# Nystrom attention and two feed-forward layers on one core: new slots for the attention of batches 2 and 3, a later start for a decode, y stores from another queue

## The chip, the core and the metric

One NeuronCore of a Trainium2 chip runs the whole program. The time is the device time of one execution in microseconds (us). Engines named here: TensorE (PE; PEld is its loading of weights), VectorE (DVE), ScalarE (ACT), GpSimd (POOL) and SyncE (SP), which here only issues DMA transfers. An engine's name with a q (SPq, ACTq) is its queue of issues.

## The reference

```python
def _attn_ref(q, k, v):                   # 4 batches, 8 heads, 576 tokens, 64 wide
    q_lm = q.reshape(B, H, 32, S // 32, D).mean(axis=3); k_lm = ...
    A = sm(q, k_lm); Bm = sm(q_lm, k_lm); C = sm(q_lm, k)      # sm: scaled softmax
    Z = Bm.T / (norm1(Bm) * norminf(Bm) + 1e-06)
    for _ in range(6):
        Z = 2 * Z - Z @ Bm @ Z
    return A @ Z @ C @ v
x = attention as (2304, 512)
h = x @ w_in                              # 512 -> 2048
x = (h * tanh(softplus(h))) @ w_out       # 2048 -> 512
h = x @ w2_in                             # 512 -> 1024
ln = layernorm(h * softmax(h)) * g_ln
out = ln @ w2_out                         # 1024 -> 512
```

The weights are float64 and come in as pairs of 32-bit words: the kernel decodes them into float32 on ScalarE, GpSimd and VectorE, and splits the result into a high and a low part, so that a product takes three matmuls.

## The kernel before

**Stages.** The prologue computes batch 0's attention and begins to decode the first layer's weights. The main loop (L859) then runs over 64 pairs p of units; a unit is one of 16 column blocks (128 wide) of the first layer's 2048, for one of 8 chunks of 288 tokens. Two chunks are a batch: batch 1 begins at pair 16, batch 2 at pair 32, batch 3 at pair 48. Chunk 0 is cut in two, so there are nine segments. After the loop comes the second layer, 18 tiles of 128 tokens.

**A pair.** gemm1(p) (12 matmuls at L623, h<-AT,u) makes h of two units. mish(p) (L648) is ScalarE's activation; gsplit(p-1) (L656 on ScalarE, L658 on VectorE) splits its result. gemm2(p-3) (24 matmuls at L671, y<-gh,hl and y<-gl,hl) sums into four PSUM banks y. At the end of a segment, evac (L685) copies each of the four banks into one of two tiles ye on ScalarE (L688) and issues its store to the DRAM buffers yd or yp on ScalarE's queue (L689).

**Attention beside it.** attn(b, g) is a generator for batch b and four of the eight heads, with 17 steps. A pair calls slot() five times (the points in '1sa.u..t2..u' at L880), so pair p holds slots 5p+1 to 5p+5. PLAN (L600) gives each generator its first slot and the slots between its steps. The tiles of one generator are single buffers shared by all, and its result AT lies in a buffer that batch b-2 used. finish_w (L508) is its last step. When both generators of a batch are done, four u steps (u_step, L605: 16 matmuls at L612, copies at L615 on ScalarE and L616 on VectorE) multiply w tiles of the first layer into u tiles; each may run as soon as the batch before has used the old u tile for the last time (may_step, L854), at the two points 'u' of a pair. A u step takes both PSUM tiles "a" of the attention.

**Second layer's weights.** The fourth u step of batch 3 is the last reader of the w tiles. At the end of that pair (or of pair 47, if that is later) the code issues the loads of w2_in (decode2, L798, into the four w tiles), closes the attention's PSUM pool and gives its memory to a second h tile (ps_x). decode works in steps: L151 on GpSimd, L154 on ScalarE, L163 and L172 on VectorE, then the split at L222 (L225) and L231 (L234). tick() (L864) does these steps while `w2n < W2R * (u - w2u)`, with W2R = 0.6, where w2u is the unit at which the loads were issued. w2_out follows in the same way into the u tiles (L914, L921).

**Order.** Instructions are written in the order of these loops. A planner puts them into each engine's queue by its own estimate of when each is ready; the place in the text is a priority. Each engine then runs its queue in order. load_y (L813), which reads yd back for the second layer, is written for pair 61 and later.

Of the kernel before, what the change touches and what calls it, by code (L numbers as in the profile page):

```python
# [27 lines left out]
def nystrom_moe_kernel(  # L28
# [13 lines left out]
    V, A, PE, G, SP = nc.vector, nc.scalar, nc.tensor, nc.gpsimd, nc.sync  # L42

    B, _, _, SH = q.shape
# [6 lines left out]
    NG = H // HG  # L51
# [10 lines left out]
    N = CR * L  # L62
# [9 lines left out]
    yd = dram.tile([P, KD, NT], F32, name="yd")  # L72
    yp = dram.tile([P, KD, N], F32, name="yp")
# [523 lines left out]
    SB = 2  # L597
    XB = 1
    YB = 2
    PLAN = {(b, g): ((6, 19.2, 97, 117, 169, 212)[2 * b + g - 2], (1.6, 1.8, 1, 2.2, 0.5, 1.5)[2 * b + g - 2]) for b in range(1, B) for g in range(NG)}  # L600
    late, anchor, atl = [], [], []
    bank_n = [0, 0]
    done = 0
# [30 lines left out]
    def gemm1(p):  # L634
        pool = ps_x[0] if ps_x and p % 2 and p < U // 2 - 1 else ps_h
        h = pool.tile([P, 2, 512], F32, tag="h", name="h")
        for e in range(2):
            s_, i = units[2 * p + e]
            b, r = divmod(segs[s_][0] * CR, R)
            w = u_q(i // 4)[:, :, :, i % 4 * P:(i % 4 + 1) * P]  # L640
            o = slice(r * L, r * L + N)
            mm3(h[:, e, 0:N], [(w[:, x, g], aw[b, g][y][:, o]) for x, y in ((0, 0), (0, 1), (1, 0)) for g in range(NG)])
        hb[p] = h[:, :, 0:N]

    def mish(p):
        h = hb.pop(p)
        s = mp.tile([P, 2, N], F32, tag="s", name="s", bufs=SB)
        A.activation(out=s, in_=h, func=AF.Mish)  # L648
        gb[p] = s

    def gsplit(p, tick):
        s = gb[p]
        gh = mp.tile([P, 2, N], F32R, tag="gh", name="gh", bufs=GB)
        gl = mp.tile([P, 2, N], F32R, tag="gl", name="gl", bufs=GLB)
        for e in range(2):
            A.activation(out=gh[:, e], in_=s[:, e], func=AF.Copy)  # L656
            tick()
            V.tensor_tensor(out=gl[:, e], in0=s[:, e], in1=f(gh[:, e]), op=ALU.subtract)  # L658
            tick()
        gb[p] = (gh, gl)  # L660

    def gemm2(p):
        s_, i = units[2 * p]
        _, i0, i1 = segs[s_]
        if i == i0:
            yb[s_] = [ps_y.tile([P, 512], F32, tag=f"y{d}", name=f"y{d}") for d in range(KD)]
        gh, gl = gb.pop(p)
        rs = [(k, s, r, e) for k, (s, r) in enumerate((("h", gh), ("l", gh), ("h", gl))) for e in range(2)]

        def add(k, s, r, e, d):  # L670
            PE.matmul(yb[s_][d][:, 0:N], lhsT=w_out(s, i + e)[:, d * P:(d + 1) * P], rhs=r[:, e],  # L671
                      start=i == i0 and e == k == 0, stop=i + 2 == i1 and e == 1 and k == 2)

        if i == i0 or i + 2 == i1:
            for d in range(KD):
                for x in rs:
                    add(*x, d)
                if i + 2 == i1:
                    evac(s_, d)
        else:  # L680
            for x in rs:
                for d in range(KD):
                    add(*x, d)

    def evac(s_, d):  # L685
        c = segs[s_][0]
        t = mp.tile([P, N], F32, tag="ye", name="ye", bufs=YB)
        A.activation(out=t, in_=yb[s_][d][:, 0:N], func=AF.Copy)  # L688
        A.dma_start(out=yp[:, d] if s_ == 0 else yd[:, d, c * N:(c + 1) * N], in_=t)  # L689

    with ExitStack():
        make_identity(nc, ident)
# [22 lines left out]
        def w1_tick(n=1):  # L715
            nonlocal done, ticks
            for _ in range(n):
                if done < NU and (ticks < 7 or atl):
                    ticks += 1
                    with tc.issue_after(atl[-1].ins) if atl else nullcontext():  # L720
                        done = next(w1, 10 ** 6)

        tasks = []
        for b in range(1, B):
            for g in range(NG):
                at, gaps = PLAN[b, g]
                tasks.append([b, at, 0, gaps, attn(b, g)])
        now = 0

        def advance(x):  # L730
            with behind(2):
                if next(x[4], "end") == "end":
                    tasks.remove(x)
                    return False
            x[1] += x[3]
            x[2] += 1
            return True
# [3 lines left out]
        for g in range(NG):  # L741
            prep, e, c, t, a = attn(0, g)
            for nm, x in (("q", prep("q")), ("k", prep("k")), ("e", e()), ("c", c()), ("t", t), ("a", a())):
                ch[f"{nm}{g}"] = x
        for nm in PSEQ.split():
            if nm == "d":
                w1_tick(1)
            elif nm == "x":
                advance(tasks[0])
                tasks[0][1] = PLAN[1, 0][0]  # L750
            elif nm not in ch and nm[0] != "w":
# [15 lines left out]
        def slot():  # L767
            nonlocal now
            now += 1
            while ahead and free_tag():  # L770
                b, g, nm = ahead.pop(0)
                load(b, g, nm)
            if late:
                with behind(0):
                    if next(late[0], "end") == "end":
                        late.pop(0)
            for x in list(tasks):
                while x[1] <= now:
                    if not advance(x):
                        break  # L780

        def finish(b):
            for x in [x for x in tasks if x[0] <= b]:
                while advance(x):
                    pass
# [56 lines left out]
        def need(side, i):  # L842
            while done <= pos[side, i] and done < NU and (ticks < 7 or atl):
                w1_tick()

        def next_step():
            b, s = steps.pop(0)
            if b == 0:
                for i in range(4 * s, 4 * s + 4):
                    need("i", i)  # L850
            finish(b)
            u_step(b, s)

        def may_step(u):  # L854
            b, s = steps[0]
            return all((b, g) in aw for g in range(NG)) and (b == 0 or last_use[b - 1, s] < u) and \
                (b > 0 or done > max(pos["i", i] for i in range(4 * s, 4 * s + 4)))

        for p in range(U // 2):  # L859
            u = 2 * p + 1  # L860
            s_, i = units[u]
            c, i0, i1 = segs[s_]

            def tick():  # L864
                nonlocal w2n
                nonlocal k4
                if done < NU:
                    k4 += 1
                    want = t0 + (3 * NU + 3 - t0) * (p + k4 / 5) / DT
                    while ticks < want and done < NU:  # L870
                        w1_tick()
                elif w2 and w2n < W2R * (u - w2u):
                    w2n += 1
                    if next(w2[0], "end") == "end":
                        w2.pop(0)

            while steps and first_use[steps[0]] <= u:
                next_step()
            k4 = 0
            for x in '1sa.u..t2..u':  # L880
                if x == '1':
                    gemm1(p)
                elif x == 'a':
                    mish(p)
                elif x == 's' and p:
                    gsplit(p - 1, tick)
                elif x == 't':
                    tick()
                elif x == '.':
                    slot()  # L890
                elif x == 'u':
                    for _ in range(US):
                        if steps and may_step(u + 1):
                            next_step()
                elif x == '2':
                    while g2 <= p - LAG:
                        need("o", units[2 * g2 + 1][1])
                        gemm2(g2)
                        g2 += 1
            if u + 1 == (NCH - 2) * NF:  # L900
                finish(B)
                att_s.close()
                tr = ctx.enter_context(tc.tile_pool(name="tr", bufs=1))
            if tr is not None and not steps and not vi:
                vi[None] = None
                w2.append(decode2(vi_pairs()))
                w2u = u
                psa_s.close()
                if HX:
                    psx_s = ExitStack()  # L910
                    ps_x.append(psx_s.enter_context(tc.tile_pool(name="ps_x", bufs=1, space=PS, side="right")))
            if c == NCH - 1:
                if i == NH - 1:
                    w2.append(decode2(vo_pairs((0, 1))))  # L914
                if i == NF - 5:
                    load_y(0)
                if i == NF - 3:
                    split_y(0)
                    load_y(1)
# [151 lines left out]
```

## Time and profile before

| | us |
|---|---|
| median of 3 runs | 659.76 (659.3 to 661.57) |
| profiled execution | 659.22 |
| its span, first to last instruction | 657.4 |
| TensorE busy | 626.1 (95%) |
| VectorE busy | 384.1 (58%) |
| ScalarE busy | 313.6 (48%) |

The span is what the trace covers; the rest of the execution's time lies around it. A share of busy time is an average over the prologue, the main loop and the second layer, which have different limits, so the stages are read one by one.

### The profile page before, as it was taken

How to read it: one execution, taken by the hardware profiler on the slowest of the kernel's cores; microseconds unless marked ns; L12 is line 12 of the kernel's file. 1: busy time of each engine (PE TensorE's matmuls, PEld its weight loads, DVE VectorE, ACT ScalarE, POOL GpSimd, SP SyncE). 2: the span in 40 equal slices, each digit the busy share in tenths (PEclk: the TensorE clock that was granted, in tenths of full speed). 3: DMA queues.
4: the chain of work that ended last, by engine and by line, in shares of the span. 5: the costliest groups of instructions: out<-in, count | busy, mean ns of one | idle time of the engine just before them, and what ended most of it. 6: DMA issues, size and time to landing. Idle time of an engine off the chain costs nothing.

```text
span 657.4 us, 11835 instructions
## 1 busy us (share of the span) xinstructions
PE 626.1 (95%) x4808; PEld 528.1 (80%) x4808; DVE 384.1 (58%) x976; ACT 313.6 (48%) x580; POOL 41.6 (6%) x21
## 2 busy tenths in 40 slices
PE   5687899999999999999997999999999999999997
PEld 2345777889889878898875999997888888888886
DVE  5899998931737235413536713457966656666560
ACT  2379985543537245424635634536534343343431
POOL 2420000000000000000005201310000000000000
PEclk9768999999999999999997999999999999999999
DMA  8998040310212010101046103213111111110001
GB/s 324 396 408 328 1 130 16 110 37 28 82 37 92 19 37 1 38 1 37 1 119 197 46 1 131 99 65 101 49 48 49 33 49 48 44 53 17 17 32 50
DMA packets 30584, 55.43 MB, mean 84 GB/s; under 512 B 3649, under 2 KB 19009, under 8 KB 30529
## 3 DMA queue, kind: packets, MB, share of 16 engines
q1 hardware_dynamic: 25344, 49.36, 21.4%
q10 hardware_dynamic: 5184, 5.31, 2.4%
q8 instruction: 38, 0.62, 0.4%
q14 instruction: 18, 0.14, 0.1%
HBM read 44.63 MB, written 10.03 MB: 83 GB/s over the span
## 4 chain that ended last, share of the span: by engine, by line
PE 85%; ACT 5%; DVE 4%; DMA 3%; issue 1%; POOL 1%; SPq 0%; POOLq 0%; ACTq 0%; DVEq 0%
PE h L623 28%; PE y L671 28%; PE po L623 15%; PE pa L612 3%; PE pt L975 2%; PE pa L298 2%; PE pa L442 2%; PE pa L353 1%; PE pa L429 1%; DMA r<-in_moe_w_in_dram 1%; POOL r L151 1%; DMA scr_w<-in_k_dram 1%; DMA r<-in_moe_w_out_dram 1%; DVE r L163 1%; ACT L648 1%
## 5 line engine op out<-in xcount | busy, mean ns | idle before, releaser
L671 PE MATMUL y<-gh,hl 128*128 128x288 f32 x1024 | 166.2, 301 | 2.4 <-ACT hl L222 1.4
L671 PEld LDWEIGHTS y<-gh,hl 128*128 128x128 f32 x1024 | 144.5, 190 | 14.1 <-issue 8.1
L623 PE MATMUL h<-AT,u 128*128 128x288 f32 x768 | 123.0, 305 | 3.7 <-ACT s L648 1.8
L623 PEld LDWEIGHTS h<-AT,u 128*128 128x128 f32 x768 | 107.9, 192 | 15.1 <-ACT u L615 4.7
L658 DVE TENSOR_TENSOR gl<-s,gh 128x288 fp32r<-128x288 f32 x128 | 55.1, 467 | 110.5 <-ACT gh L656 48.2
L623 PE MATMUL h<-hl,yb 128*128 128x512 f32 x432 | 103.2, 394 | 0.3 <-DVE s L948 0.3
L623 PEld LDWEIGHTS h<-hl,yb 128*128 128x128 f32 x432 | 79.7, 188 | 17.1 <-issue 1.0
L671 PE MATMUL y<-gl,hl 128*128 128x288 f32 x512 | 89.6, 298 | 0.0
L623 PE MATMUL po<-hl,lh 128*128 128x512 f32 x288 | 89.1, 390 | 0.0
L671 PEld LDWEIGHTS y<-gl,hl 128*128 128x128 f32 x512 | 75.0, 189 | 4.2 <-issue 3.0
L656 ACT ACTIVATE gh<-s 128x288 fp32r<-128x288 f32 x128 | 50.7, 436 | 55.6 <-PE y L671 55.3
L648 ACT ACTIVATE s<-h 128x576 f32<-128x576 f32 x64 | 41.6, 650 | 65.9 <-PE h L623 58.8
L623 PEld LDWEIGHTS po<-hl,lh 128*128 128x128 f32 x288 | 53.9, 188 | 11.1
L623 PE MATMUL po<-hl,ll 128*128 128x512 f32 x144 | 56.1, 390 | 0.0
L151 POOL TENSOR_SCALAR r<-r 128x1024 f32<-128x1024 f32 x10 | 31.6, 3162 | 363.4 <-DMA r<-in_moe_w_in_dram 303.2
L127 ACT ACTIVATE yb<-y 128x512 fp32r<-128x512 f32 x18 | 11.4, 632 | 51.0 <-PE h L623 49.5
L951 ACT ACTIVATE e<-s,st 128x1024 f32<-128x1024 f32 x18 | 20.7, 1151 | 29.6 <-DVE st L950 29.5
L943 DVE TENSOR_REDUCE st<-h 128x1 f32<-128x1024 f32 x18 | 22.0, 1223 | 21.1 <-PE h L623 16.3
L945 ACT ACTIVATE e<-h,st 128x1024 f32<-128x1024 f32 x18 | 20.1, 1117 | 28.7 <-DVE st L944 28.7
L612 PE MATMUL pa<-w,W 64*32 64x512 f32 x256 | 28.3, 643 | 5.2 <-DVE u L616 4.0
L623 PEld LDWEIGHTS po<-hl,ll 128*128 128x128 f32 x144 | 27.0, 188 | 5.6
L616 DVE TENSOR_TENSOR u<-pa,u 128x512 fp32r<-128x512 f32 x32 | 21.0, 686 | 13.9 <-ACT u L615 13.6
(168 smaller groups left out, 676.6 us busy)
## 6 DMA issues: line engine op xcount, KB each, us to landing
r<-in_moe_w_in_dram SPq DMA_DIRECT2D x8, 1024.0 KB, 8.7
ro<-in_moe_w_out_dram SPq DMA_DIRECT2D x8, 1024.0 KB, 17.8
yd<-ye ACTq DMA_DIRECT2D x32, 144.0 KB, 1.8
y<-yd SPq DMA_DIRECT2D x18, 256.0 KB, 3.1
out_dram<-ob SPq DMA_DIRECT2D x18, 256.0 KB, 2.0
w<-in_moe_w_in_dram SPq DMA_DIRECT2D x4, 1024.0 KB, 10.7
v<-in_v_dram SPq DMA_DIRECT2D x8, 512.0 KB, 4.1
r<-in_moe_w_out_dram SPq DMA_DIRECT2D x4, 1024.0 KB, 4.9
```

The source lines that it names most:

```text
L151: G.tensor_scalar(out=x, in0=x, scalar1=2.0 ** -112, scalar2=None, op0=ALU.mult)
L298: PE.matmul(out[r], lhsT=lhsT[r], rhs=rhs[r], start=True, stop=True)
L612: mm = PE.matmul(po[g][h * L:(h + 1) * L], lhsT=wb[b][r, g, h * L:(h + 1) * L], rhs=w[r, h], start=True, stop=True)
L616: V.tensor_tensor(out=u[:, 1, g], in0=po[g], in1=f(u[:, 0, g]), op=ALU.subtract))
L623: PE.matmul(o, lhsT=a, rhs=b_, start=i == 0, stop=i == n - 1)
L648: A.activation(out=s, in_=h, func=AF.Mish)
L656: A.activation(out=gh[:, e], in_=s[:, e], func=AF.Copy)
L658: V.tensor_tensor(out=gl[:, e], in0=s[:, e], in1=f(gh[:, e]), op=ALU.subtract)
L671: PE.matmul(yb[s_][d][:, 0:N], lhsT=w_out(s, i + e)[:, d * P:(d + 1) * P], rhs=r[:, e], start=i == i0 and e == k == 0, stop=i + 2 == i1 an ...
L943: V.tensor_reduce(out=st[:, 0:1], in_=h, op=ALU.max, axis=AX.X)
L945: A.activation(out=e, in_=h, func=AF.Exp, bias=st[:, 1:2], accum_out=st[:, 2:3])
L951: A.activation(out=e, in_=s, func=AF.Square, bias=st[:, 4:5], accum_out=st[:, 5:6])
```

## The change

PLAN gets new first slots and gaps for batches 2 and 3 and keeps those of batch 1: (2, 0) moves from slot 97 to 82 with a gap of 1 as before, (2, 1) from 117 with 2.2 to 102 with 1, (3, 0) from 169 with 0.5 to 162 with 1, (3, 1) from 212 with 1.5 to 182 with 1. The decode of w2_in may start its steps six units (three pairs) later than its loads. The stores of y are issued by SyncE and not by ScalarE, which means that they wait there for ScalarE's copy.

```diff
-    PLAN = {(b, g): ((6, 19.2, 97, 117, 169, 212)[2 * b + g - 2], (1.6, 1.8, 1, 2.2, 0.5, 1.5)[2 * b + g - 2]) for b in range(1, B) for g in range(NG)}
+    W2D = 6
+    PLAN = {(1, 0): (6, 1.6), (1, 1): (19.2, 1.8), (2, 0): (82, 1.0), (2, 1): (102, 1.0),
+            (3, 0): (162, 1.0), (3, 1): (182, 1.0)}
@@ evac
-        A.dma_start(out=yp[:, d] if s_ == 0 else yd[:, d, c * N:(c + 1) * N], in_=t)
+        SP.dma_start(out=yp[:, d] if s_ == 0 else yd[:, d, c * N:(c + 1) * N], in_=t)
@@ main loop
                 w2.append(decode2(vi_pairs()))
-                w2u = u
+                w2u = u + W2D
```

## Rows read from the trace of the kernel before

**Rows 1.** The page: busy shares, granted clock in 40 slices, mish's group.
```profile
PE 626.1 (95%) x4808; PEld 528.1 (80%) x4808; DVE 384.1 (58%) x976; ACT 313.6 (48%) x580; POOL 41.6 (6%) x21
...
PEclk9768999999999999999997999999999999999999
...
L648 ACT ACTIVATE s<-h 128x576 f32<-128x576 f32 x64 | 41.6, 650 | 65.9 <-PE h L623 58.8
```
**Rows 2.** Stages: from:to, length, busy time (instructions) by engine, clock, DMA.
```profile
161.65:188.74 27.09, 27.07 (x302) 23.44 (x301) 15.77 (x47) 13.48 (x30) 0.00 (x0) 1.00 0.23 76
193.52:250.02 56.50, 56.50 (x546) 48.52 (x545) 25.58 (x65) 27.43 (x55) 0.00 (x0) 1.00 0.13 43
250.02:276.99 26.97, 26.97 (x301) 23.45 (x300) 13.36 (x45) 13.42 (x30) 0.00 (x0) 1.00 0.07 23
276.99:300.89 23.90, 23.90 (x182) 23.90 (x181) 4.14 (x10) 7.15 (x15) 0.00 (x0) 1.00 0.00 1
300.89:341.97 41.08, 40.51 (x405) 33.52 (x403) 18.23 (x53) 20.46 (x41) 0.00 (x0) 1.00 0.15 45
341.97:362.50 20.53, 16.32 (x113) 12.11 (x106) 13.52 (x19) 11.45 (x18) 9.68 (x3) 0.83 0.63 202
395.91:425.54 29.63, 29.00 (x219) 28.77 (x218) 13.42 (x20) 14.80 (x29) 7.34 (x3) 1.00 0.36 127
```
**Rows 3.** Timeline, 330 to 362 us: start, length, instruction, idle before and releaser.
```profile
335.51 0.38 PE L508 MATMUL pa<-MT,Cv 128*128 128x128 f32 x2
...
335.92 0.58 SPq L815 DMA_DIRECT2D y<-yd  x1
...
337.76 0.40 SPq L798 DMA_DIRECT2D r<-in_moe_w_in_dram  x1
...
343.84 8.02 SPq L798 DMA_DIRECT2D r<-in_moe_w_in_dram  x2
344.52 1.16 ACT L154 ACTIVATE r<-r 128x1024 uint32<-128x1024 uint8 x1 [1.58 <-DMA r<-in_moe_w_in_dram]
344.67 2.91 POOL L151 TENSOR_SCALAR r<-r 128x1024 f32<-128x1024 f32 x1 [298.30 <-DMA r<-in_moe_w_in_dram]
...
347.62 1.23 DVE L163 SCALAR_TENSOR_TENSOR r<-r 128x1024 uint32<-128x1024 uint32 x1 [3.83 <-POOL r L151]
...
349.50 1.93 PE L612 MATMUL pa<-w,W 64*32 64x512 f32 x8 [4.00 <-DVE u L616]
```
**Rows 4.** Chain that ended last, in order of time: start, length, what.
```profile
337.76 6.74 DMA r<-in_moe_w_in_dram
...
397.70 4.98 DMA r<-in_moe_w_out_dram
```
**Rows 5.** Timeline of SyncE's queue: the last load of batch 2.
```profile
124.70 0.33 SPq L289 DMA_DIRECT2D k<-in_k_dram  x1
```
**Rows 6.** Timeline of TensorE, 130.5 to 137 us: starts of pairs 13 and 14.
```profile
130.60 1.75 PE L623 MATMUL h<-AT,u 128*128 128x288 f32 x12
...
136.58 0.69 PE L623 MATMUL h<-AT,u 128*128 128x288 f32 x4
```
**Rows 7.** Timeline, 395 to 465 us: the later decode on VectorE.
```profile
405.82 1.23 DVE L163 SCALAR_TENSOR_TENSOR r<-r 128x1024 uint32<-128x1024 uint32 x1 [4.04 <-POOL r L151]
```
**Rows 8.** Tile ye: its stores, what it waits for, who waits, landing.
```profile
L689 ACTq DMA_DIRECT2D yd<-ye x32: 326/327/557, 139.6 to 447.1; - x32
...
  DMA yd<-ye: 3.4, 4
...
  PE y L671: 0.6, 1
...
DMA to landing us min/median/max: 1.7/1.8/3.9
```
**Rows 9.** Timeline after the loop: the second layer's third tile.
```profile
451.57 6.87 PE L623 MATMUL h<-hl,yb 128*128 128x512 f32 x28 [0.31 <-DVE s L948]
```
**Rows 10.** SyncE's waits: queue and line, releaser, us in total, times, longest.
```profile
SPq L815 <- PE pa L508: 71.7, 1, 71.7
```

## The prediction

> **What bounds the kernel now.** I read the page first: TensorE is busy for 95% of the span, no other compute engine for more than 58%, and its granted clock sits at 0.9 or more from slice 5 on but for slice 22 [rows 1]. A busy TensorE is not one at its peak, so the next view is the table by stages, cut where a pair's first matmul starts [rows 2]. In the stretch 276.99 to 300.89 us five pairs run with nothing beside them: 23.90 us, so 4.78 us for a plain pair of 12 first-layer and 24 second-layer matmuls. That is the floor; TensorE bounds these pairs and nothing waits. All other stretches of the table are read as so many pairs at 4.78 us and the rest:
>
> - 161.65 to 188.74, pairs 19 to 22, attention of batch 2, heads 0 to 3 (slot 97, one slot a step): 27.09 - 4 x 4.78 = 7.97 us.
> - 193.52 to 250.02, pairs 24 to 32, its heads 4 to 7 (slot 117, 2.2 slots a step) and batch 2's four u steps: 56.50 - 9 x 4.78 = 13.48 us.
> - 250.02 to 276.99, pairs 33 to 36, batch 3, heads 0 to 3 (slot 169, half a slot a step): 26.97 - 4 x 4.78 = 7.85 us.
> - 300.89 to 362.50, pairs 42 to 49 (41.08 and 20.53 us), batch 3, heads 4 to 7 (slot 212), its four u steps and the first decode of the second layer: 61.61 - 8 x 4.78 = 23.37 us.
>
> The four sums make 52.67 us. The last is the odd one, so the third view is the timeline there [rows 3]. The attention ends at 335.5 (L508), in the first slot of pair 47, and batch 3 starts at pair 48: all four u steps have to follow each other within 21 us. A u step frees one of the w tiles, so the second layer's first load leaves at once, at 337.76, and takes 6.74 us [rows 4]; ScalarE stands 1.58 us for it, GpSimd then takes 2.91 us, and VectorE's L163 stands 3.83 us for GpSimd. Behind L163 in VectorE's queue is L616 of a u step, and TensorE's next u step needs the PSUM tile that L616 reads: it waits 4.00 us at 349.50. The granted clock of this stretch falls to 0.83 [rows 2], so after TensorE has stood still some of its matmuls run at the lower level (1.2 GHz).
>
> **One thing about order.** Queues aren't in the order of the program's text. load_y(0) is written in pair 61 and issued at 335.92, in pair 47, right behind the last reader of the attention's memory [rows 3]. The planner lets an instruction go ahead when its engine is free and its inputs are there. So a later place in the text, which is all that W2D gives, lowers a decode's priority and needn't delay it. I count W2D itself at nothing; what should move the decode out of the way is that the attention ends earlier.
>
> **The change, part by part.** The base of the sum is the profiled execution, 659.22 us (span 657.4 us and 1.8 around it); the median of the runs is 659.76, 0.54 above.
>
> Slots. A pair has five slots, and an attention 17 steps. The new places put batch 2 into pairs 16 to 19 and 20 to 23, and batch 3 into pairs 32 to 35 and 36 to 39, none overlapping. Nothing of the matmul work goes away. Inputs: the last load of batch 2 left at 124.70 [rows 5], under a plan that doesn't change up to there, and its scores come in pair 20, some 45 us later; batch 3's loads follow the steps that free the tiles, which come earlier too. The AT tiles of batch b-2 are last read in pairs 15 and 31, just ahead of pairs 16 and 32, and are written only late in an attention, so no wait is added. Each attention is priced by the two that ran close together: (7.97 + 7.85) / 2 = 7.91, four of them 31.6 us.
>
> U steps. They can now run as soon as the batch before has read its last u column block: pairs 25, 27, 29, 31 and 41, 43, 45, 47, one every 9.6 us. The nearest row is a single u step in pair 13: 136.58 - 130.60 - 4.78 = 1.20 us [rows 6]. Eight make 9.6 us.
>
> Decode of the second layer's first weights (four items). Each load can leave two pairs after the one before, when its w tile is freed, or all four at the end of pair 47 as written. Bounds: 0 if all hides, as nearly in the later decode; 8.7 us if the collision stays as it is (the 20.53 us of pairs 48 and 49 [rows 2] less 9.56 for two pairs and 2.4 for two u steps, which is 8.6, rounded up). For the value: the later decode of w2_out waited likewise (VectorE 4.04 us for GpSimd at 405.82 [rows 7]), and six pairs with three of its items took 29.63 us [rows 2], 0.95 over the floor. What hid it is that no u step ran there and that h had two PSUM tiles. Here h has one until the last u step: ScalarE may be late by some 2.5 us (24 of a plain pair's 36 matmuls, 3.19 us, less 0.65 for L648 [rows 1]), and a 1.58 us wait with 1.16 of L154 [rows 3] is 2.74, so a little over for each of four items. I take 1.5 us in all, near the later decode.
>
> The y stores. 36 issues of 0.33 us leave ScalarE's queue [rows 8], 11.8 us in all, from an engine that is busy for 48% [rows 1]; TensorE waited for an evacuation once, 0.6 us, so the gain is 0 to 0.6. What it adds: SyncE waits for ScalarE's copy, and behind that wait stand loads (q, k, v, weights, y), which have time, as batch 2's 45 us above; and the store stands behind loads in SyncE's queue. Only two ye tiles exist, so the third evacuation of a segment waits for the first store to land (3.4 us in all over 36 [rows 8]). Evacuations fall in pairs 6, 14, 18, 26, 34, 42, 50, 58 and after the loop. With loads leaving as tiles come free, the nearest in front is the first weight load, in pair 41, some 6 us ahead of the stores of pair 42, against a landing of 5.0 to 6.7 us [rows 4]: a collision of under 1 us, within ScalarE's cover. At the end the path is tight: ye, the exponential, L948, then matmuls that waited 0.31 us [rows 9], and y loads share SyncE's queue with the stores: -0.3 to +1. I take +0.3 for the whole part.
>
> The Trainium skill ("DMA: Bandwidth & Descriptors", Queues, rings and completion order) speaks against this part: SyncE and ScalarE own a row of rings each, and a DMA engine takes turns between rows packet by packet, so that a store on ScalarE's row shares with a running load, while on SyncE's row it comes behind it. The trace fits: on ScalarE's row the slowest store landed after 3.9 us, median 1.8 [rows 8]. No row shows SyncE's. By that rule the second rival below is what happens wherever a load is in front.
>
> **The sum**: 659.22 - 52.67 + 31.6 + 9.6 + 1.5 + 0.3 = 649.55 us; the median stands 0.54 higher: 650.0 us.
>
> **Rivals.**
> First, the decode goes on colliding: the planner puts an L163 ahead of an L616 or of a gl, and GpSimd's 2.9 us and a load's tail are paid again in pairs 42 to 49. For it: the text's place didn't hold the decode back before [rows 3]. Against it: u steps are 9.6 us apart, so a late L616 has a whole pair to spare. Price: 4 to 8.7 in place of 1.5: 652.5 to 657, say 655.
>
> Second, slower: y behind the weights. If the four loads leave together at the end of pair 47, as written, they hold SyncE's queue for 4 x 6.74 = 27 us [rows 4]. The first stores of pair 50 come 2 x 4.78 + 1.6 + 0.8 = 12 us after that and land at 28.8 and not at 13.8. ScalarE stands some 15 us in the third evacuation, with mish behind it; one pair of cover, 4.8 us, is against that, so TensorE loses 10, and about 3.5 more at the lower clock (0.83 over 20.5 us [rows 2]): 650 + 13.5 = 663.5. It decides when more than about two loads are in front of an evacuation. Against it: the same loads left one by one in the trace, at 337.76 and after [rows 3]. The same price holds if SyncE sits in a wait ahead of a store; it sat 71.7 us for L508 once [rows 10], but with L508 in pair 39 that ends ahead of the evacuation in pair 42.
>
> Third, no change: the attentions are won, but the decode keeps its 8.6 us (650.0 - 1.5 + 8.6 = 657.1) and a collision or two of the stores with a load cost 1 to 3: 658 to 660.
>
> **How the numbers follow.** Forecast 650.0 with 0.60 (its own range 646 to 653: the decode at 0, the stores at -0.6, and attentions up to half a microsecond cheaper each; upwards the stores at +1 and the decode at 3.5). Below 646: 0.04. First rival 0.18, third 0.08, second 0.10. Range 646 to 657: it leaves out the third, the second, and what lies below 646, about 0.2. This kernel's measurement tells a difference of about 0.3%, 2 us. Faster 0.82, same 0.08, slower 0.10.
>
> **What would show it.** Pairs 24, 26, 28, 30 and 40, 42 (but for its u step and evacuation) at 4.78 us; four attentions of about 8 us each in pairs 16 to 23 and 32 to 39; u steps singly, 1.2 us each; no wait of several microseconds of L612 for L616; the clock at 1.00 from 320 to 360 us. ScalarE's wait for a y store over 3.4 us in total, or a landing of a y store over 5 us, speaks for the second rival; VectorE's L163 standing for GpSimd with TensorE late behind it, for the first. I'm wrong if the attentions cost clearly more than 8 us each in their new places, or if the stretch of pairs 41 to 50 is still over 8 us above its floor and u steps.

## The result, and the profile after

The median fell from 659.53 us (four runs, 658.61 to 661.57) to 652.67 us (four runs, 651.14 to 653.6), a ratio of 0.989 with a 95% interval of 0.9859 to 0.992: 6.9 us less, where 9.8 were forecast. The profiled execution of the new kernel took 651.14 us with a span of 649.2, the shortest of its four. Lines from L606 on have moved by two (L616 is L618, L671 is L673, L689 is L691).

The stages after, cut where a pair's first matmul starts (from:to, length, busy time by engine, clock, DMA); they answer to [rows 2]:

```profile
146.89:173.99 27.10, 27.08 (x301) 23.44 (x300) 15.77 (x47) 13.37 (x31) 0.00 (x0) 1.00 0.25 78
173.99:201.10 27.11, 27.09 (x301) 23.46 (x300) 15.78 (x47) 12.96 (x28) 0.00 (x0) 1.00 0.21 68
201.10:244.26 43.16, 43.16 (x355) 39.14 (x353) 11.78 (x24) 17.24 (x36) 0.00 (x0) 1.00 0.06 21
244.26:271.11 26.85, 26.85 (x301) 23.46 (x300) 13.32 (x45) 12.94 (x29) 0.00 (x0) 1.00 0.07 24
271.11:297.95 26.84, 26.84 (x301) 23.45 (x300) 13.32 (x45) 13.07 (x28) 0.00 (x0) 1.00 0.03 9
297.95:313.53 15.58, 15.58 (x127) 14.57 (x126) 6.45 (x12) 6.00 (x12) 0.44 (x1) 1.00 0.45 126
313.53:339.06 25.53, 23.53 (x178) 21.12 (x177) 12.84 (x18) 13.67 (x27) 7.37 (x3) 0.93 0.34 107
```

Rows one, two, four and five are the four attentions, four pairs each: 7.98, 7.99, 7.73 and 7.72 us over a floor of 4.78 a pair. Row three is eight pairs with batch 2's four u steps: 4.9 over, 1.2 each. Row six, pairs 40 to 42, has one u step, and TensorE loses nothing else there (15.58 - 14.34 = 1.24). Row seven, pairs 43 to 46, has two u steps and the decode: 25.53 - 19.12 - 2.4 = 4.0 us over, with a clock of 0.93. Pair 47 is a plain pair and a u step (6.00 us). From pair 50 to the first matmul of the second layer the loop takes 70.98 us (71.00 before), and the second layer 223.6 (223.9).

What is in row seven shows in the timeline there (start, length, instruction, idle before and releaser):

```profile
306.81 0.99 SPq L800 DMA_DIRECT2D r<-in_moe_w_in_dram  x1
...
312.94 1.15 ACT L154 ACTIVATE r<-r 128x1024 uint32<-128x1024 uint8 x1 [1.76 <-DMA r<-in_moe_w_in_dram]
313.09 2.95 POOL L151 TENSOR_SCALAR r<-r 128x1024 f32<-128x1024 f32 x1 [266.84 <-DMA r<-in_moe_w_in_dram]
...
313.53 1.76 PE L625 MATMUL h<-AT,u 128*128 128x288 f32 x12
313.98 0.69 ACT L690 ACTIVATE ye<-y 128x288 f32<-128x288 f32 x2
314.39 6.46 SPq L691 DMA_DIRECT2D yd<-ye  x4
...
316.07 1.23 DVE L163 SCALAR_TENSOR_TENSOR r<-r 128x1024 uint32<-128x1024 uint32 x1 [6.16 <-POOL r L151]
...
317.34 1.23 DVE L172 SCALAR_TENSOR_TENSOR cc<-r 128x1024 uint32<-128x1024 uint32 x1
...
318.68 1.06 ACT L222 ACTIVATE hl<-cc 128x1024 fp32r<-128x1024 f32 x1 [3.35 <-DVE cc L172]
319.64 0.69 ACT L690 ACTIVATE ye<-y 128x288 f32<-128x288 f32 x2
...
320.09 0.79 PE L673 MATMUL y<-gh,hl 128*128 128x288 f32 x4 [2.00 <-ACT ye L690]
...
322.39 2.66 PE L625 MATMUL h<-AT,u 128*128 128x288 f32 x12
```

It is a chain: the first weight load, GpSimd's L151, VectorE's L163 and L172, ScalarE's L222, and behind L222 in ScalarE's queue the third and fourth evacuation of pair 42. TensorE's next segment stands 2.00 us for a y bank. The first two evacuations had already waited behind L154, which stood 1.76 us for the load. In the trace before, the same chain ended in L616 and a u step [rows 3]; no u step waits for it now.

The stand of 2.00 us is half of the 4.0. Behind it TensorE works without a gap, but at a lower granted clock; this is the stretch up to the end of pair 44's gemm1:

```profile
320.09:325.05 4.96, 4.96 (x26) 4.96 (x27) 2.98 (x5) 2.54 (x6) 0.00 (x0) 0.66 0.73 211
```

The mean of 0.66 means that most of the stretch ran at the lower level (1.2 GHz). Pair 43's twelve gemm1 matmuls took 1.76 us, pair 44's 2.66. Estimated from this row, the clock cost 4.96 x 0.34 = 1.7 us, and pair 44's 0.9 us over its floor is this and no wait.

The y stores of the new kernel, to be read against [rows 8]: their issues, who waited for them, and the time to landing.

```profile
L691 SPq DMA_DIRECT2D yd<-ye x32: 319/338/747, 139.2 to 439.7; - x32
...
  ACT ye L690: 3.0, 4
...
DMA to landing us min/median/max: 1.7/1.8/4.1
```

They land as they did from the other queue.

### The profile page after: what moved, and what is told of

The parts are those of the page before. It is cut to its first block, busy times and chain, and to the rows that moved or that the text cites. A ratio compares the mean times of both kernels' runs of the same rounds, so it can differ in the third digit from the quotient of the medians.

```text
span 649.2 us, 11859 instructions
## 1 busy us (share of the span) xinstructions
PE 621.0 (96%) x4808; PEld 527.2 (81%) x4808; DVE 382.2 (59%) x976; ACT 307.4 (47%) x576; POOL 38.7 (6%) x21
## 4 chain that ended last, share of the span: by engine, by line
PE 88%; ACT 4%; DVE 4%; DMA 2%; issue 1%; POOL 0%; SPq 0%; ACTq 0%; POOLq 0%
PE h L625 30%; PE y L673 30%; PE po L625 15%; PE pa L614 3%; PE pt L977 2%; PE pa L298 2%; PE pa L442 2%; PE pa L429 1%; PE pa L353 1%; DVE r L163 1%; DMA scr_w<-in_k_dram 1%; DMA r<-in_moe_w_out_dram 1%; ACT L650 1%; PE pa L410 1%; POOL r L151 0%
## 5 line engine op out<-in xcount | busy, mean ns | idle before, releaser
L673 PE MATMUL y<-gh,hl 128*128 128x288 f32 x1024 | 164.4, 300 | 4.4 <-ACT ye L690 2.6
L673 PEld LDWEIGHTS y<-gh,hl 128*128 128x128 f32 x1024 | 143.3, 188 | 16.9 <-issue 8.0
L625 PE MATMUL h<-AT,u 128*128 128x288 f32 x768 | 124.6, 307 | 3.6 <-ACT s L650 1.8
L625 PEld LDWEIGHTS h<-AT,u 128*128 128x128 f32 x768 | 109.3, 193 | 12.5 <-ACT u L617 4.7
L660 DVE TENSOR_TENSOR gl<-s,gh 128x288 fp32r<-128x288 f32 x128 | 53.3, 453 | 91.4 <-ACT gh L658 40.4
L673 PE MATMUL y<-gl,hl 128*128 128x288 f32 x512 | 90.2, 298 | 0.0
L673 PEld LDWEIGHTS y<-gl,hl 128*128 128x128 f32 x512 | 74.8, 188 | 3.7 <-issue 2.1
L151 POOL TENSOR_SCALAR r<-r 128x1024 f32<-128x1024 f32 x10 | 29.1, 2914 | 357.8 <-DMA r<-in_moe_w_in_dram 292.9
L163 DVE SCALAR_TENSOR_TENSOR r<-r 128x1024 uint32<-128x1024 uint32 x12 | 15.3, 1273 | 34.8 <-POOL r L151 34.8
L618 DVE TENSOR_TENSOR u<-pa,u 128x512 fp32r<-128x512 f32 x32 | 20.9, 686 | 14.9 <-ACT u L617 14.6
```

Of the source, the lines that this page charges most:

```text
L151: G.tensor_scalar(out=x, in0=x, scalar1=2.0 ** -112, scalar2=None, op0=ALU.mult)
L163: V.scalar_tensor_tensor(out=t[:, :, 0], in0=t[:, :, 1], scalar=3, in1=t[:, :, 0], op0=ALU.logical_shift_left, op1=ALU.bitwise_or)
L618: V.tensor_tensor(out=u[:, 1, g], in0=po[g], in1=f(u[:, 0, g]), op=ALU.subtract))
L625: PE.matmul(o, lhsT=a, rhs=b_, start=i == 0, stop=i == n - 1)
```

## The experiments

Each kernel was timed beside the kernel before; the last column is the loop from the start of pair 16 to the second layer's first matmul, read off its one trace, which leaves out the prologue and the second layer.

| kernel | median us | ratio to before (95%) | pairs 16 to 63, us |
|---|---|---|---|
| before | 659.5 to 660.7 | 1 | 286.18 |
| changed kernel | 652.67 | 0.989 (0.9859 to 0.992) | 278.71 |
| e1_plan | 653.08 | 0.9896 (0.9879 to 0.9913) | 279.44 |
| e2_stores | 657.97 | 0.9969 (0.9952 to 0.9987) | 285.65 |
| e3_batch2 | 658.54 | 0.9984 (0.9968 to 0.9999) | 284.69 |
| e4_batch3 | 654.12 | 0.99 (0.9883 to 0.9917) | 279.67 |
| e5_pin | 648.10 | 0.9818 (0.9794 to 0.9842) | 275.55 |
| e6_pin2 | 646.75 | 0.9802 (0.9778 to 0.9825) | 274.78 |
| e7_held | 646.62 | 0.9799 (0.9775 to 0.9822) | 274.64 |
| e8_w2d0 | 653.05 | 0.9886 (0.986 to 0.9911) | 279.51 |
| e9_row_sp | 663.62 | 1.0043 (1.0022 to 1.0063) | 291.81 |
| e10_row_act | 654.06 | 0.9909 (0.9871 to 0.9946) | 280.63 |
| e11_held_old | 652.78 | 0.9886 (0.9869 to 0.9902) | 280.67 |
| e12_held_acty | 649.23 | 0.9828 (0.9806 to 0.985) | 275.04 |

The theory: the earlier attention carries the gain, W2D nothing, the stores next to nothing, and what is lost against the forecast is the decode's place in ScalarE's queue. The rivals are those of the prediction and those named below.

**One part at a time.** e1_plan:

```diff
-    PLAN = {(b, g): ((6, 19.2, 97, 117, 169, 212)...
+    PLAN = {(1, 0): (6, 1.6), (1, 1): (19.2, 1.8), (2, 0): (82, 1.0), (2, 1): (102, 1.0),
+            (3, 0): (162, 1.0), (3, 1): (182, 1.0)}
```

> The kernel before with the new slots alone (y stores stay on ScalarE's queue, W2D is not there). My theory: the slots carry the gain; 52.67 us over the floor become 31.4 for four attentions, 9.7 for u steps and about 4 for the decode, so some 7.5 us less than before, 652 us. Rival: a good part comes from the y stores' move; then this one gains 5 us or less.

It measured 653.08 us at a ratio of 0.9896: the whole gain of the change, to within the intervals. e2_stores:

```diff
-        A.dma_start(out=yp[:, d] if s_ == 0 else ...
+        SP.dma_start(out=yp[:, d] if s_ == 0 else ...
```

> The kernel before with the y stores on SyncE's queue and nothing else. My theory: within 0.7 us of before on either side, as TensorE waited once for an evacuation, 0.6 us. Rival: 2 us or more either way, a gain from ScalarE's 11.8 us of issues or a loss behind loads.

A miss on the time: 0.9969 is 2.0 us less, 0.9 to 3.2 by the interval. Its trace has only 0.5 of that in the loop (285.65 against 286.18). The following rows are that stretch of the kernel before and of e2_stores; the busy times of all engines are alike.

```profile
147.32:433.50 286.18, 280.74 (x2502) 254.18 (x2501) 126.50 (x294) 133.80 (x266) 23.74 (x8) 0.99 0.18 59
```

```profile
148.05:433.70 285.65, 280.53 (x2502) 254.52 (x2501) 125.79 (x294) 134.18 (x266) 23.09 (x8) 0.99 0.18 59
```

Two other pairs of kernels differ in the stores alone (and in W2D, which does nothing, as e8_w2d0 shows): e1_plan and the changed kernel (0.9896 and 0.989, 0.4 us) and e12_held_acty and e7_held below (0.9828 and 0.9799, 1.9 us). The intervals overlap in both. So the move gains 0.4 to 2 us in the timed runs, and only e2_stores tells it from nothing. The loops of the three pairs differ by 0.4 to 0.7 us, no more than two traces of equal queues do (0.8 us, below); where the gain lies stays open.

e3_batch2 and e4_batch3 move one batch each:

```diff
-((6, 19.2, 97, 117, 169, 212)[...], (1.6, 1.8, 1, 2.2, 0.5, 1.5)[...])
+((6, 19.2, 82, 102, 169, 212)[...], (1.6, 1.8, 1, 1, 0.5, 1.5)[...])     # e3_batch2
+((6, 19.2, 97, 117, 162, 182)[...], (1.6, 1.8, 1, 2.2, 1, 1)[...])       # e4_batch3
```

> The kernel before with batch 2's slots alone (82 and 102, one slot a step). My theory: 21.45 us over the floor for its two attentions and four u steps become 7.98 + 7.99 + 4.8 = 20.8, so 0.7 us less, 659 us. Rival: close steps of heads 4 to 7 save more, 2 us.

> The kernel before with batch 3's slots alone (162 and 182, one slot a step). My theory: nearly the whole gain is here, 7.85 + 23.37 us over the floor become 7.7 + 7.7 + 4.8 + 4.0 = 24.2, so 7 us less, 652.7 us, with the wait of L612 for L616 gone. Rival: half of it or less, 656 us or more.

Batch 2 alone gave 1.1 us, batch 3 alone 6.6. The gain is where the prediction's table had its odd row: heads 4 to 7 of batch 3 ended in the last pair before their batch began (the first slot of pair 47).

**W2D.** e8_w2d0:

```diff
-    W2D = 6
+    W2D = 0
```

> The changed kernel with W2D = 0. My theory: the planner had let the decode steps ahead anyway, so nothing changes, within 0.5 us of the changed kernel, and the trace shows the same stalls in pairs 43 and 44. Rival: without the three pairs the decode collides as before, 655 us or more.

Every engine's queue holds the same instructions in the same order as in the changed kernel; 653.05 us, and the stretch of pairs 43 to 46 is as long as there:

```profile
315.40:340.96 25.56, 23.36 (x178) 21.11 (x177) 12.88 (x18) 13.87 (x27) 7.47 (x3) 0.93 0.34 106
```

W2D does nothing. The two traces also say how far one trace goes: with equal queues the loop took 279.51 and 278.71 us.

**The decode's place.** e5_pin and e6_pin2 order ScalarE's decode steps behind evacuations:

```diff
+        evs[s_] = A.activation(out=t, in_=yb[s_][d][:, 0:N], func=AF.Copy)
...
-                    if next(w2[0], "end") == "end":
+                    with tc.issue_after(evs[5].ins):           # e6_pin2: evs[7] for w2_out
+                        if next(w2[0], "end") == "end":
```

> The changed kernel, with w2_in's decode steps on ScalarE held behind the last evacuation of pair 42. My theory: the changed kernel loses 2.9 us in pair 43 and 0.9 in pair 44 because the first item's L154 waits for its load, and its L222 for VectorE, ahead of evacuations in ScalarE's queue; held behind them, pairs 43 and 44 lose at most 0.5 us, so some 3.3 us less than the changed kernel, 649.4 us. Rival: the delay comes from the y stores in SyncE's queue or from the load itself; then nothing changes, 652.7 us.

> As e5_pin, and w2_out's decode steps on ScalarE held behind the last evacuation of pair 58. My theory: pair 59's 0.84 us goes too, 648.6 us. Rival: the later start pushes the decode of w2_out into the second layer, and its first tiles wait: 650 us or more.

The rows are pairs 43 and 44 of e5_pin and pair 59 of e6_pin2:

```profile
315.54:326.33 10.79, 10.79 (x90) 9.78 (x89) 7.22 (x9) 7.76 (x15) 5.07 (x2) 1.00 0.42 136
```

```profile
392.93:397.72 4.79, 4.79 (x38) 4.79 (x37) 3.12 (x4) 2.91 (x7) 0.23 (x1) 1.00 0.57 168
```

10.79 is two plain pairs and a u step to 0.03 us, and 4.79 a plain pair (pair 59 took 5.6 us in the changed kernel): both losses are gone, and the clock stays at 1.00. In e5_pin the queues of TensorE, GpSimd and SyncE hold the same as in the changed kernel in the same order, so loads and stores go out as before. ScalarE's differs by the two steps L154 and L222 that were held. VectorE's order moved with them: two gl steps now stand ahead of L163, and the u copies ahead of L172. TensorE's wait in the changed kernel ended with ScalarE's evacuation, so ScalarE's order is the cause of that stand; what VectorE's order adds was not taken apart. In e6_pin2 one load of w2_out also moved up in SyncE's queue. 648.10 and 646.75 us.

e7_held does on ScalarE what W2D was to do:

```diff
+        msh[0] = A.activation(out=s, in_=h, func=AF.Mish)
...
+                    with tc.issue_after(msh[0].ins):
+                        if next(w2[0], "end") == "end":
```

> The changed kernel, with each decode step on ScalarE held behind the mish that stands just before it in the text, so that the decode of w2_in does start three pairs behind its loads (pair 50 and later). My theory: no load is waited for, the u steps are over and h has two tiles, so the decode costs under 1.5 us, 650 us. Rival: it is then too close to the end of the loop and the second layer's first matmuls wait for it: 653 us or more.

646.62 us, 3.4 us less than expected. Pairs 43 to 47, pairs 48 to 50 and pairs 51 to 62:

```profile
315.36:342.94 27.58, 27.58 (x231) 24.56 (x230) 8.92 (x16) 11.89 (x25) 8.97 (x3) 1.00 0.36 109
342.94:357.28 14.34, 14.34 (x110) 14.34 (x109) 3.71 (x7) 5.85 (x11) 2.91 (x1) 1.00 0.12 45
357.28:414.67 57.39, 57.39 (x435) 57.39 (x434) 30.43 (x43) 31.06 (x58) 8.05 (x3) 1.00 0.23 75
```

27.58 is five pairs and three u steps (27.5), 14.34 three plain pairs, 57.39 twelve (57.36). GpSimd's L151 still runs as each load lands (8.97 us in the first row); ScalarE's first L154 comes at 354.84, in pair 50, and VectorE's steps behind it. The decode costs TensorE nothing here. e6_pin2 and e7_held are equally fast and the best kernels of this study, 0.9% under the changed one; e6_pin2 shows that an early decode is as good, if no evacuation stands behind it.

e11_held_old asks whether that alone would have done, with the old slots; e12_held_acty takes the stores back in e7_held:

```diff
 # e7_held with the old PLAN and the stores on ScalarE's queue (e11_held_old)
 # e7_held with the stores on ScalarE's queue (e12_held_acty)
+        A.dma_start(out=yp[:, d] if s_ == 0 else ...
```

> The kernel before (old slots, y on ScalarE's queue) with its decode held as in e7_held, three pairs and more behind the loads. It asks whether a held decode alone would have done. My theory: the decode's 8.6 us of pairs 48 and 49 nearly go and the attentions keep their price, so some 7.5 us less than before, 652.5 us, and the new slots are worth 4 us on top of it (e7_held). Rival: the four u steps, still bunched, are what waits there; then it gains 3 us or less.

> The kernel of e7_held with the y stores back on ScalarE's queue: what the stores' move is worth when nothing else stalls. My theory: within 0.7 us of e7_held. Rival: 2 us, as e2_stores measured.

e12_held_acty is a miss on the time like e2_stores: 2.6 us above e7_held (1.9 by the ratios) and not 0.7, but 0.4 in the loop.

e11_held_old: 652.78 us, as much as the whole change by its median; its loop is 5.5 us shorter than before, the changed kernel's 7.5. Pairs 48 and 49 of it, which answer to the sixth of [rows 2], and two of TensorE's instructions there:

```profile
341.64:357.55 15.91, 14.98 (x113) 11.84 (x106) 6.42 (x11) 6.71 (x13) 8.69 (x3) 0.89 0.81 264
```

```profile
348.76 1.06 PE L613 MATMUL pa<-w,W 64*32 64x512 f32 x8 [0.61 <-DVE u L617]
...
350.15 1.06 PE L613 MATMUL pa<-w,W 64*32 64x512 f32 x8 [0.33 <-DVE u L617]
```

15.91 - 9.56 - 2.4 leaves 3.95 us where there were 8.6: 4.6 were the decode's. Of the rest the rows show two waits of the u steps' matmuls (L613) for the copy of the step before (L617), 0.61 and 0.33 us, and a granted clock of 0.89, an estimated 1.7 us; three u steps follow each other there, from 340.62 on, and share two PSUM tiles with their copies. What is left of it was not traced. The 652.5 us expected came out; the new slots and stores are worth about 6 us on top of it (e7_held) and not 4. So the change and a held decode cure overlapping parts of one stall, and together give 13.8 us (e7_held).

**Y behind copies.** e9_row_sp and e10_row_act measure the second rival. They move 8 MB more than the kernel needs:

```diff
+        if s_ in (3, 4) and d == 0:            # pairs 26 and 34, behind the first store
+            with tc.issue_after(st.ins):
+                for k_ in range(4):            # 1 MB each, DRAM to DRAM
+                    dum[s_] = SP.dma_start(out=scrd[:, k_], in_=w2_in[...])
 # stores d = 1 to 3 behind these: on SyncE (e9_row_sp), on ScalarE (e10_row_act)
```

> The changed kernel with extra work: in pairs 26 and 34, behind the first y store of the segment and ahead of the other three, SyncE issues four copies of 1 MB each from one DRAM buffer to another. It measures the second rival. By its price the second store lands 20 to 27 us late, the fourth evacuation waits for its tile, and each place costs 10 to 20 us: 675 to 690 us. Rival: 16 DMA engines serve all alike, a store lands within 4 us, and the time is within 3 us of the changed kernel.

> As e9_row_sp, with the other three stores of those two segments on ScalarE's queue. If a queue's own transfers stand behind each other and those of two queues take turns, these stores land within some 5 us and the time is within 4 us of the changed kernel. Rival: the copies hold the DMA engines for all, and it loses as much as e9_row_sp.

The first place in e9_row_sp, from its timeline, and the landing of its stores (L692 is evac's copy, L697 its store, L701 the four copies, L675 gemm2):

```profile
216.46 0.33 SPq L697 DMA_DIRECT2D yd<-ye  x1
...
216.84 2.99 SPq L701 DMA_DIRECT2D scrd<-in_moe_w_in_dram  x4
...
219.93 16.36 SPq L697 DMA_DIRECT2D yd<-ye  x3
...
235.53 0.41 ACT L692 ACTIVATE ye<-y 128x288 f32<-128x288 f32 x1 [13.40 <-DMA yd<-ye]
...
235.99 1.33 PE L675 MATMUL y<-gh,hl 128*128 128x288 f32 x4 [5.61 <-ACT ye L692]
```

```profile
DMA to landing us min/median/max: 1.7/1.8/15.5
```

and in e10_row_act the stores on ScalarE's queue (issues, KB, median us to landing) and the slowest landing of all:

```profile
yd<-ye ACTq DMA_DIRECT2D x6, 144.0 KB, 8.7
```

```profile
DMA to landing us min/median/max: 1.7/1.9/10.6
```

The mechanism is there: a store behind 4 MB in the same queue lands after up to 15.5 us, ScalarE stands 13.40 us for the tile, and TensorE 5.61. The price was half of what I gave it: against the changed kernel the ratio rises by 1.5%, 10 us for two places, 5 each and not 10 to 20. In the two traces the places are unequal: pairs 27 to 30 take 7.7 us more than in the changed kernel, pairs 35 to 39 4.3. The store landed about 18.6 us after the first copy's issue, where the second rival puts 27 us on four loads, so this prices a somewhat shorter jam. From the other queue the same stores landed after 8.7 us (median), and the kernel lost about 1.3 us (0.9909 against 0.989, whose intervals overlap; 1.9 us in the loop). Both expectations on that landing were off: on the one queue the store came sooner than 20 us, and on the other it still took several times the usual 1.8 us. The Trainium skill's rule ("DMA: Bandwidth & Descriptors", Queues, rings and completion order), that a DMA engine takes turns between the two rows, fits these landings in kind. In the changed kernel itself no load was in front of an evacuation for long, and the slowest store landed after 4.1 us.

## Why the prediction was right, and where it was off

In terms of the profiled execution the sum said 649.55 us and the trace gave 651.14; the median came out 2.7 us above the forecast 650.0 and inside the range. The main mechanism, the earlier attention, was right. For the decode it was the first rival that happened, at the low end of its price (4 us), and 652.67 lies in that rival's 652.5 to 657 as well as in the forecast's own 646 to 653: the trace tells them apart, not the number. That the miss isn't larger is in part luck: pair 16 began 0.4 us earlier than in the trace before, for which the sum has no term.

- **Four attentions at 7.91 us, 31.6.** Measured 7.98, 7.99, 7.73, 7.72: 31.4. The price of two groups with close steps carried over to the new places.
- **Eight u steps at 1.20, 9.6.** They came singly at 1.2, in the pairs that the prediction named.
- **The decode at 1.5, between 0 and 8.7.** It took 4.0 (pairs 43 to 46), and that is the term that was mis-sized: 2.5 us. Of the 4.0, 2.0 are a stand of TensorE and an estimated 1.7 the lower clock behind it, which the term did not count. The mechanism was that of the first rival, L163 standing for GpSimd (6.16 us at 316.07) with TensorE late behind it, but what came late was not L616 or a gl: it was an evacuation. What I had not followed is the next engine. I looked for what stands behind L163 on VectorE and what stands behind L154 on ScalarE, and took h as the only thing at stake; but L222 stands in ScalarE's queue for VectorE too, and the evacuations stand behind L222. I had put pair 42's evacuation and the first load 6 us apart and drew from it only that their transfers wouldn't meet. Their instructions met on ScalarE. e5_pin settles it.
- **W2D at nothing.** Right, and exactly so (e8_w2d0). The reason given, that a place in the text doesn't hold an instruction back, is what e7_held confirms from the other side: held in fact on ScalarE, the decode costs TensorE nothing.
- **The stores at +0.3 us.** The sign was wrong by e2_stores, 2.0 us less (0.9 to 3.2). The other two pairs point the same way without telling it from nothing, and so do the loops (0.4 to 0.7 us). At the end of the loop, where I feared for the tight path, nothing was lost: the second layer took 223.6 us, 0.3 less.
- **What would show it.** The waits of L612 for L616 are gone. The clock was to be 1.00 between 320 and 360 us; it is 0.93 between 313.53 and 339.06, a consequence of the decode's stall, since e5_pin without the stall has 1.00 in pairs 43 and 44. L163 stood for GpSimd with TensorE late behind it, the sign named for the first rival. No y store landed after more than 4.1 us, and ScalarE's wait for them was 3.0 us in all, so the second rival's signs are absent.
- **The second rival** didn't occur because the loads left one by one as tiles came free, at 306.81, 320.95, 330.98 and 341.97, each behind a u step. At e9_row_sp's two places a jam of its kind cost 5 us each, not the 13.5 of the prediction. TensorE had more cover than one pair: 13.40 us of ScalarE's standing made it wait 5.61, as it still had a gemm1, a u step and gemm2 matmuls to do.

## What to carry to other kernels

When a step of a side job is moved, follow its wait through every engine that it passes, to the end: each engine in the chain has its own queue behind it, and the cost lands where something urgent stands behind the last link. Where a planner orders the queues, a later place in the program is a wish; an order between two instructions of one engine is what holds, and it is worth reading the queues before counting on a delay. Work that must end before a stage (an attention, its u steps) belongs early enough that the next stage's preparation doesn't meet it.

## What was not expected of the hardware

The start of pair 16 lay between 145.12 and 148.27 us in the fourteen traces, though the kernels hardly differ up to there; two kernels with equal queues had it at 146.89 and 147.92. So some 3 us of difference between single executions come from the prologue, and a span of one trace can't be held against another's to better than that; the loop can, to about 0.8 us. The price of a collision moves as well: pair 43, whose floor with its u step is 6.00 us, took 8.87 to 9.84 us in the changed kernel, e1_plan, e4_batch3 and e8_w2d0.
